# Splitting the first expert's weights: fewer pieces in the attention loop and all of them on GpSimd, the last three in the transition, and key tiles of half the size

## The chip, the cores and the metric

The kernel runs on one core of a Trainium2 chip. The metric is the device time of one execution in microseconds (us): median, lowest and highest of several runs. The profile is of one execution of its own. The core has a matrix engine (TensorE; PE in the profile, its weight loads PEld), a vector engine (VectorE, DVE), a scalar engine (ScalarE, ACT), GpSimd (POOL) and a queue engine (SyncE, SP) that mostly starts DMA transfers. Each engine runs its own instructions in the order in which they were written and waits on semaphores for the others. The matrix engine writes its results into PSUM, from which ScalarE and VectorE read; GpSimd works on SBUF alone.

## The reference

Attention with pooled keys and values, and then a mixture of eight experts of which each row takes one:

```
k_p = k.reshape(B, H, S // 8, 8, 64).mean(axis=3)       # v_p likewise; B = H = 8, S = 576
scores = q @ k_p.T / 8;  attn = softmax(scores)          # 72 pooled keys
x = (attn @ v_p) as (4608 rows, 512)
e = argmax(x @ w_gate)                                   # one of 8 experts for each row
out[row] = gate[row] * (relu(x[row] @ w1[e]) @ w2[e])    # w1[e] 512 x 1024, w2[e] 1024 x 512
```

## The kernel before

**Attention.** `attention` (L79 to L649) works on 36 tiles of 128 query rows, in four groups of nine (`NT` = 9; the number within the group is `KIND(t)`, L55). Two of the 8 sequences of `B` form one group. The program is written out by hand in the order in which each engine shall run it; the loop over `t` (L543) is a software pipeline. In one step, called tile t here, it does in this order:

- loads of later keys, values and queries by SP (L546 to L555), and the load of a raw weight piece (L565);
- `p_transpose(t)` (L278): TensorE transposes tile t's attention weights in six pieces (L283), ScalarE copies them out in two copies (`pt`, L284);
- `scores(t + 2)` (L257): 32 small matmuls into `pS` (L263), then on VectorE the maximum (`mx`, L267) and the subtraction (`sd`, L270), both read from PSUM;
- `q_transpose(t + 3)` (L250): four transposes and a copy by ScalarE;
- in some steps the transposes of the next group's pooled keys and values (`kv_transpose`, L176, with four copies by ScalarE) or the expansion of the values with the gate's columns (`v_expand`, L202, with one copy);
- `weights(t + 2)` (L274): the exponentials on ScalarE;
- `weigh(t)` (L291): TensorE multiplies the weights by the values into `pU` (L299), and `scale(t)` (L302) on VectorE divides by the sums (`r`, `lh`, `xe`, L311 to L315).

**Routing.** Tiles are routed in batches of three (`SIZES`, L38), the last of them at tiles 2, 5, ..., 20, 23, 26, 29, 32. `route` (L329) appends to VectorE's order: the logits' sum `rg` (L374), its maximum `rm` (L375), the difference `rd` (L376) and the key `rk` (L378) directly, and after the next tile's `mx` the maximum `rn` (L379) and the choice `ro` (L346). `rd`, `rk` and `ro` have two operands in SBUF. In the next tile, after `weigh`, TensorE counts the rows of each expert from `ro` (L356, L359), VectorE adds the carry (L361, L362), and GpSimd multiplies (`rp`, L388). One tile later VectorE reduces to the row numbers (`rf`, L389), and GpSimd scatters the batch to DRAM, for each tile one cast (`ix`, L368) and one indirect DMA (L407).

**The first expert's weights.** The experts' products are made in split form: a high part (`fp32r`, a cast by ScalarE) and a low part (raw minus high). The first expert's w1 and w2 are eight pieces of 128 x 1024 (512 KB each): pieces 0 to 3 are w1, 4 to 7 are w2. With `W0T` = 21, piece i is loaded by SP in tile 18 + i into one of four buffers that the raw keys and values use as well (`w_load`, L415). It is split at the end of tile 21 + i (`w_split`, L421): the cast on ScalarE (L424), the subtraction on GpSimd where the tile's number divides by 3 (pieces 0, 3, 6), else on VectorE (L425).

**The transition.** From tile 29 on, the first unit's rows are loaded back (`x_load`, L433, eight transfers by SP) and split (`x_split`, L450). `x_open` (L444), at tile 31, gives the memory of the buffers for raw data to the tiles `X` and `H`. After the loop TensorE runs six of eight hidden pieces of the first unit (`multiply`, L461, L463; each piece is 12 matmuls into one of three banks), and ScalarE and VectorE take out the first four (`hidden`, L467: L468, L469). In between VectorE computes the experts' tables (`plan`, L652), which calls `more_hidden` (L640) in the middle and `last_hidden` (L644) at its end. Then all engines meet at L728, where SP waits for each in turn, and `experts` (L712) begins: up to 16 units of at most 512 rows, with their own splits of later experts' weights (L1061 on ScalarE, L1069 on VectorE and GpSimd). At its start GpSimd clears `Y` (L1338).

**The keys.** `kTs` (L91) holds the pooled keys transposed, with the even heads in partitions 0 to 63 and the odd ones in 64 to 127. Each has its own 72 of 144 columns; the other 72 stay zero and are read by no matmul. VectorE clears the first of the two tiles at the start (L101), GpSimd the second (L493).

Of the kernel before, what the change touches and what calls it, by code (L numbers as in the profile page):

```python
# [10 lines left out]
F32 = mybir.dt.float32  # L11
# [4 lines left out]
ALU = mybir.AluOpType  # L16
AX = mybir.AxisListType

P = 128
# [3 lines left out]
SK = S // POOL  # L23
# [10 lines left out]
NB = 3  # L34
# [6 lines left out]
W0T = 21  # L41
# [9 lines left out]
def f32(a):  # L51
    return a.bitcast(F32)
# [26 lines left out]
def attention(ctx, outer, tc, q, k, v, wg, w1v, w2v, xs, W, cst, carry, tab, banks):  # L79
    nc = tc.nc  # L80
# [7 lines left out]
    e2 = early.enter_context(tc.tile_pool(name="e2", bufs=2, side="right", reuse_waits="tile"))  # L88
    kraw = early.enter_context(tc.tile_pool(name="akv", bufs=4, side="right", reuse_waits="tile"))

    kTs = [one.tile([P, 2, 4, 2 * SK], F32, name=f"kT{i}") for i in range(2)]  # L91
    kvp = e1.tile([P, NT, P], F32, name="kvp")
    vT = e1.tile([P, H * KP + KW], F32, name="vT")
    Vs = [one.tile([P, 2, 2, 5, D + NE + 1], F32, name=f"V{i}") for i in range(2)]
# [3 lines left out]
    colv = e1.tile([P, 5], F32, name="colv")  # L98
    exs = [one.tile([P, NB, NE + 1], F32, name=f"ex{i}") for i in range(2)]
    nc.vector.memset(kvp, 0.0)  # L100
    nc.vector.memset(kTs[0], 0.0)  # L101
    nc.vector.memset(vT, 0.0)

    for t in Ps:
# [71 lines left out]
    def kv_transpose(g, i, bank, what="kv", take=nc.scalar.copy):  # L176


        for c in range(3):
            nc.tensor.transpose(bank[:, c * P : (c + 1) * P], kvp[:, 3 * i + c, :], ident)  # L180
        m = bank[:, 0 : 3 * P].rearrange("p (c bj hp k) -> p hp bj k c", c=3, hp=2, k=8)
        for hp in range(2):
            rk, rv = slice(64 * hp, 64 * hp + 64), slice(64 - 64 * hp, 128 - 64 * hp)
            ko = kTs[g % 2].rearrange("p b j (hp k c) -> p hp (b j) k c", hp=2, c=9)
            vo = vT[:, 0 : 2 * H * KP].rearrange("p (bj hp x) -> p hp bj x", hp=2, x=KP)[:, :, :, 0:SK].rearrange("p hp b (k c) -> p hp b k c", c=9)
            if "k" in what:
                take(out=ko[rk, hp, :, :, 3 * i : 3 * i + 3], in_=m[0:64, hp])
            if "v" in what:
                take(out=vo[rv, hp, :, :, 3 * i : 3 * i + 3], in_=m[64:128, hp])

# [66 lines left out]
    def scores(t):  # L257
        g = t // NT
        for j in range(4):
            for p0, b in [(0, 0), (64, 1)] if KIND(t) == 4 else [(0, parts(t)[0][2]), (64, parts(t)[0][2])]:  # L260
                for hp in range(2):
                    r = slice(64 * hp, 64 * hp + 64)
                    nc.tensor.matmul(pS[p0 : p0 + 64, hp, j * SK : (j + 1) * SK], lhsT=qT[t][r, j * P + p0 : j * P + p0 + 64],  # L263
                                     rhs=kTs[g % 2][r, b, j, hp * SK : (hp + 1) * SK], start=True, stop=True, skip_group_check=True)
        s4 = pS[:, :, 0:288].rearrange("p a (h x) -> p a h x", h=4)
        mx = p2.tile([P, 2, 4], F32, tag="mx", name=f"mx{t}")
        nc.vector.tensor_reduce(out=mx, in_=s4, axis=AX.X, op=ALU.max)  # L267
        weave()
        sd = p2.tile([P, 2, 4, SK], F32, tag="sd", name=f"sd{t}")
        nc.vector.tensor_tensor(out=sd, in0=s4, in1=mx.unsqueeze(3).to_broadcast([P, 2, 4, SK]), op=ALU.subtract)  # L270
        weave(1, True)
        sds[t] = sd
# [140 lines left out]
    w0 = {}  # L413

    def w_load(i):  # L415

        raw = kraw.tile([P, 1024], F32, tag="raw", name=f"w0_{i}")
        nc.sync.dma_start(out=raw.rearrange("p (c f) -> p c f", c=4 if i < 4 else 2), in_=load_piece(w1v, w2v, 0, i))
        w0[i] = raw

    def w_split(i):  # L421
        raw = w0.pop(i)
        c, a = slice((i % 4) * 1024, (i % 4 + 1) * 1024), 0 if i < 4 else 2
        nc.scalar.copy(out=W[:, a, c], in_=raw)  # L424
        (nc.gpsimd if (W0T + i) % NB == 0 else nc.vector).tensor_tensor(out=W[:, a + 1, c], in0=raw, in1=f32(W[:, a, c]), op=ALU.subtract)  # L425

    def clear_rows():
        for s in range(4):  # L430
# [13 lines left out]
    def x_open():  # L444
        early.close()
        m1 = outer.enter_context(tc.tile_pool(name="m1", bufs=1, side="right", reuse_waits="tile"))
        u0["H"] = m1.tile([P, 2, 8, 512], F32R, name="H")
        u0["X"] = m1.tile([P, 2, 4, 512], F32R, name="X")

    def x_split(s):  # L450
        bank, o = (pm, pq)[s % 2], slice(s * P, (s + 1) * P)
# [9 lines left out]
    def multiply(n):  # L461
        for f, k, i in products[:n]:
            nc.tensor.matmul(pH[f % 3], lhsT=w1s(W[:, int(i == 2)], f, k), rhs=u0["X"][:, int(i == 1), k, :],  # L463
                             start=k + i == 0, stop=k == 3 and i == 2, skip_group_check=True)
        del products[:n]

    def hidden(f):  # L467
        nc.scalar.activation(out=u0["H"][:, 0, f, :], in_=pH[f % 3], func=AF.Relu)  # L468
        nc.vector.scalar_tensor_tensor(out=u0["H"][:, 1, f, :], in0=pH[f % 3], scalar=0.0, in1=f32(u0["H"][:, 0, f, :]), op0=ALU.max, op1=ALU.subtract)  # L469
# [20 lines left out]
    clear_rows()  # L490
    gate_rhs()
    sums()
    nc.gpsimd.memset(kTs[1], 0.0)  # L493

    def warm(n):
        for _ in range(n):
# [46 lines left out]
    for t in range(total):  # L543
# [14 lines left out]
        for at, n, *gj in adds:  # L558
            if at == t:
# [2 lines left out]
                    pieces[third] = kv_pool(*gj, vec)  # L562
                halves.extend(pieces[third][:n])
                del pieces[third][:n]
        if 0 <= t - W0T + 3 < 8:  # L565
            w_load(t - W0T + 3)
        if 0 < t < total - 2:
            p_transpose(t)
        if 2 < t + 2 < total:
# [41 lines left out]
        for bt, (t0, nb) in enumerate(batches):  # L611
            if t == t0 + nb - 1:
                route(bt)
        if 0 <= t - W0T < 8:
            w_split(t - W0T)
        if t == total - 7:
            x_load()
        if t == total - 5:
# [20 lines left out]

    def more_hidden():  # L640
        hidden(1)
        multiply(12)

    def last_hidden():  # L644
        for f in range(2, AF_EV):
            hidden(f)
            multiply(12)

    return u0, more_hidden, last_hidden  # L649
# [876 lines left out]
```

## Time and profile before

| | us |
|---|---|
| median of 3 runs | 627.91 |
| lowest, highest | 627.83, 630.01 |
| profiled execution, its own time | 627.27 |
| its span, first to last instruction | 625.7 |
| attention to the last step's x split and the transition, up to L860 | 0 to 188.76 |
| experts | 188.76 to 625.70 |

| engine | busy us | share of the span |
|---|---|---|
| PE | 599.4 | 96% |
| PEld | 511.0 | 82% |
| DVE | 347.9 | 56% |
| ACT | 241.4 | 39% |
| POOL | 241.7 | 39% |

A row of a timeline gives the start and the length in us from the span's start, the engine, the line, the operation, the tile that is written and those that are read with their shapes, how many instructions were merged, and in brackets how long the engine stood idle before and what ended that. A row of a source line's view gives the minimum, median and maximum length in ns, and the first and last start. A row by windows gives the busy time (and count) of each engine in a stretch.

### The profile page before, as it was taken

The numbers are of one execution on the slowest core, as the hardware profiler recorded it, in microseconds if no ns is written. First come the engines' busy times: TensorE is split into PE (matmuls) and PEld (weight loads), VectorE is DVE, ScalarE is ACT, GpSimd is POOL, SyncE is SP. The second block draws the span as 40 slices with busy tenths as digits, with TensorE's granted clock in tenths as the row PEclk, the third lists the DMA queues.
The fourth block names the chain that finished last, engine by engine and source line by source line (L and its number), as shares of the span: only waits on it lengthen the run. The fifth ranks groups of instructions, "written<-read, shape, count | busy, mean of one in ns | idle before, by whom it ended". The sixth has DMA issues, their size and how long they took to land.

```text
span 625.7 us, 13480 instructions
## 1 busy us (share of the span) xinstructions
PE 599.4 (96%) x4412; PEld 511.0 (82%) x4412; DVE 347.9 (56%) x731; ACT 241.4 (39%) x453; POOL 241.7 (39%) x288
## 2 busy tenths in 40 slices
PE   6989999999999999999999999999999999999995
PEld 5778989888877878789897888888898888888994
DVE  6699898888751324368475532755137764133220
ACT  2567776877411114065363411523024641021110
POOL 7447657644321122367444411152116861101101
PEclk9999999999999999999999999999999999999999
DMA  9999998982334931506967853064304353100001
GB/s 321 367 279 267 306 262 263 252 253 70 126 111 145 288 112 54 186 25 179 289 185 230 273 115 87 2 211 136 105 35 143 89 146 71 56 0 37 36 4 53
DMA packets 93938, 96.48 MB, mean 154 GB/s; under 512 B 43102, under 2 KB 74846, under 8 KB 93792
## 3 DMA queue, kind: packets, MB, share of 16 engines
q1 hardware_dynamic: 85808, 74.27, 42.3%
q0 software_dynamic: 7440, 20.50, 9.2%
q8 instruction: 61, 1.00, 0.7%
q14 instruction: 85, 0.70, 0.4%
q10 hardware_dynamic: 544, 0.02, 0.0%
HBM read 72.68 MB, written 26.00 MB: 158 GB/s over the span
## 4 chain that ended last, share of the span: by engine, by line
PE 76%; DVE 9%; issue 5%; POOL 4%; ACT 2%; DMA 2%; DVEq 0%; SPq 0%; ACTq 0%; POOLq 0%
PE pU L882 32%; PE pP L860 20%; PE pq L860 10%; PE pU L299 4%; DMA XE<-in_v_dram 2%; PE pP L283 2%; PE pP L463 2%; POOL dispatched L407 2%; PE pS L263 1%; PE pq L253 1%; DVE raw L172 1%; DVE mx L267 1%; POOL raw L172 1%; PE pm L207 1%; DVE xe L315 1%
## 5 line engine op out<-in xcount | busy, mean ns | idle before, releaser
L882 PE MATMUL pU<-W,H 128*128 128x512 f32 x912 | 216.3, 397 | 0.0
L882 PEld LDWEIGHTS pU<-W,H 128*128 128x128 f32 x912 | 171.3, 188 | 41.0
L860 PE MATMUL pP<-X,W 128*128 128x512 f32 (+3 forms) x748 | 143.2, 345 | 4.2 <-DVE W L1069 1.5
L860 PEld LDWEIGHTS pP<-X,W 128*128 128x128 f32 x748 | 122.7, 188 | 21.4 <-issue 3.0
L1351 POOL DMA_INDIRECT out_dram<-Y,GT x51 | 52.8, 1036 | 192.5 <-DVE Y L1174 179.3
L1069 POOL TENSOR_TENSOR W<-ST,W 128x1024 fp32r<-128x1024 f32 x30 | 77.8, 2607 | 88.1 <-ACT W L1061 88.1
L971 ACT ACTIVATE H<-pP 128x512 fp32r<-128x512 f32 (+1 forms) x67 | 36.0, 538 | 191.0 <-PE pP L860 154.7
L1174 DVE TENSOR_SCALAR Y<-pU,GT 128x512 f32<-128x512 f32 x36 | 27.0, 749 | 107.6 <-PE pU L882 106.2
L992 DVE SCALAR_TENSOR_TENSOR H<-pP,H 128x512 fp32r<-128x512 f32 (+2 forms) x73 | 42.2, 580 | 72.0 <-ACT H L971 70.3
L860 PE MATMUL pq<-X,W 128*128 128x512 f32 (+3 forms) x364 | 73.0, 348 | 2.4 <-issue 1.7
L860 PEld LDWEIGHTS pq<-X,W 128*128 128x128 f32 x364 | 60.0, 188 | 11.7 <-issue 2.5
L1061 ACT CAST W<-ST 128x1024 fp32r<-128x1024 f32 x56 | 57.3, 1054 | 6.7 <-DMA ST<-in_moe_w_dram 6.7
L299 PE MATMUL pU<-V,pt 110*128 110x146 f32 (+3 forms) x468 | 56.7, 283 | 1.4 <-ACT pt L284 0.8
L299 PEld LDWEIGHTS pU<-V,pt 110*128 110x128 f32 (+3 forms) x468 | 51.4, 179 | 3.1 <-ACT pt L284 1.8
L407 POOL DMA_INDIRECT dispatched<-xe,ix x36 | 39.8, 1107 | 18.2 <-POOL ix L368 9.8
L971 ACT ACTIVATE H<-pq 128x512 fp32r<-128x512 f32 (+1 forms) x33 | 17.9, 542 | 70.0 <-PE pq L860 68.5
L1069 DVE TENSOR_TENSOR W<-ST,W 128x1024 fp32r<-128x1024 f32 x26 | 40.5, 1560 | 4.6 <-ACT W L1061 4.1
L992 DVE SCALAR_TENSOR_TENSOR H<-pq,H 128x512 fp32r<-128x512 f32 (+2 forms) x35 | 20.8, 595 | 30.6 <-ACT H L971 29.8
L284 ACT COPY pt<-pP 110x384 f32<-110x384 f32 x72 | 30.9, 481 | 6.5 <-PE pP L283 5.8
L1049 DVE TENSOR_TENSOR X<-pS,X 128x512 fp32r<-128x512 f32 x34 | 21.9, 685 | 19.0 <-ACT X L1034 11.3
L276 ACT ACTIVATE P<-sd 128x576 f32<-128x576 f32 x36 | 24.8, 689 | 19.9 <-DVE sd L270 18.0
L172 POOL TENSOR_TENSOR raw<-raw 128x768 f32<-128x768 f32 (+1 forms) x18 | 26.3, 1460 | 13.5 <-DMA raw<-in_v_dram 12.8
(185 smaller groups left out, 625.4 us busy)
## 6 DMA issues: line engine op xcount, KB each, us to landing
ST<-in_moe_w_dram SPq DMA_DIRECT2D x56, 512.0 KB, 6.3
raw<-in_k_dram SPq DMA_DIRECT2D x12, 768.0 KB, 7.3
raw<-in_v_dram SPq DMA_DIRECT2D x11, 768.0 KB, 10.1
XE<-dispatched SPq DMA_DIRECT2D x104, 64.0 KB, 2.5
qa<-in_q_dram SPq DMA_DIRECT2D x24, 256.0 KB, 7.5
w<-in_moe_w_dram SPq DMA_DIRECT2D x8, 512.0 KB, 5.3
XE<-dispatched SPq DMA_DIRECT2D x15, 256.0 KB, 4.3
qa<-in_q_dram SPq DMA_DIRECT2D x2, 1024.0 KB
```

The lines of the kernel that those rows point to most:

```text
L172: return lambda: eng.tensor_tensor(out=out, in0=raw[:, :, 0:n], in1=raw[:, :, n : 2 * n], op=ALU.add)
L284: take(out=pt[t][a][0:R], in_=pPs[a][0:R, 0 : 3 * P])
L299: nc.tensor.matmul(pu[p0 : p0 + n, a, h * VW : (h + m) * VW], lhsT=pt[t][a][0:r, c % 3 * P + p0 : c % 3 * P + p0 + n], rhs=Vs[g % 2][0:r, ...
L407: apart(nc.gpsimd.indirect_dma_start(out=xs, out_offset=bass.IndirectOffsetOnAxis(ap=at, axis=0), in_=rows, in_offset=None))
L860: r = pe.matmul(out=pH[g % 3][:, :m], lhsT=w1s(w, f, k), rhs=x, start=i == 0, stop=i == len(passes) - 1)
L882: r = pe.matmul(out=pY[:, s % 2, :], lhsT=h, rhs=w[:, k * 512 : (k + 1) * 512], start=start and i == 0, stop=stop and i == len(ps) - 1, sk ...
L971: act.activation(out=HH[:, f, o], in_=src[:, o], func=AF.Relu).then_inc(Q["A_h"], 1)
L992: return dve.scalar_tensor_tensor(out=dst[:, f, to], in0=src[:, at], scalar=0.0, in1=f32(HH[:, f, at]), op0=ALU.max, op1=ALU.subtract)
L1061: act.copy(out=(W1H if i < 4 else W2H)[:, o], in_=ST[:, i, :]).then_inc(Q["A_s1" if i < 4 else "A_s2"], 1)
L1069: eng.tensor_tensor(out=(W1L if i < 4 else W2L)[:, o], in0=ST[:, i, :], in1=f32((W1H if i < 4 else W2H)[:, o]), op=ALU.subtract).then_inc( ...
L1174: r = dve.tensor_scalar(out=Y[:, s, :], in0=a, scalar1=gate, scalar2=None, op0=ALU.mult)
L1351: pool.indirect_dma_start(out=out, out_offset=bass.IndirectOffsetOnAxis(ap=GT[:, u, s, 1:2].bitcast(I32), axis=0), in_=Y[:, s, :], in_offs ...
```

## The change

1. Only pieces 0 to 4 are split in the loop, one every second tile: at the ends of tiles 21, 23, 25, 27 and 29, loaded three tiles ahead (18, 20, ..., 26). All five subtractions are on GpSimd.
2. Pieces 5, 6 and 7 are loaded by SP at tiles 32, 33 and 34 into a new tile `late`, which lies behind `H` and `X`. In the transition ScalarE casts piece 5 after the second hidden piece and pieces 6 and 7 after the third; VectorE subtracts 5 and 6 after the third hidden piece and 7 after the fourth.
3. Each key tile has 72 columns instead of 144: the even and the odd heads use the same columns in their own partitions. The two clears go.

```
-    kTs = [one.tile([P, 2, 4, 2 * SK], F32, name=f"kT{i}") for i in range(2)]
+    kTs = [one.tile([P, 2, 4, SK], F32, name=f"kT{i}") for i in range(2)]
-    nc.vector.memset(kTs[0], 0.0)
...
-            ko = kTs[g % 2].rearrange("p b j (hp k c) -> p hp (b j) k c", hp=2, c=9)
+            ko = kTs[g % 2].rearrange("p b j (k c) -> p (b j) k c", c=9)
-                take(out=ko[rk, hp, :, :, 3 * i : 3 * i + 3], in_=m[0:64, hp])
+                take(out=ko[rk, :, :, 3 * i : 3 * i + 3], in_=m[0:64, hp])
...
-                                     rhs=kTs[g % 2][r, b, j, hp * SK : (hp + 1) * SK], ...
+                                     rhs=kTs[g % 2][r, b, j, :], ...
...
-        raw = kraw.tile([P, 1024], F32, tag="raw", name=f"w0_{i}")
+        raw = kraw.tile([P, 1024], F32, tag="raw", name=f"w0_{i}") if i < 5 else u0["late"][:, i - 5]
...
-    def w_split(i):
-        raw = w0.pop(i)
-        c, a = slice((i % 4) * 1024, (i % 4 + 1) * 1024), 0 if i < 4 else 2
-        nc.scalar.copy(out=W[:, a, c], in_=raw)
-        (nc.gpsimd if (W0T + i) % NB == 0 else nc.vector).tensor_tensor(out=W[:, a + 1, c], in0=raw, in1=f32(W[:, a, c]), op=ALU.subtract)
+    def w_high(i):
+        nc.scalar.copy(out=W[:, 0 if i < 4 else 2, (i % 4) * 1024 : (i % 4 + 1) * 1024], in_=w0[i])
+
+    def w_low(i, eng):
+        c, a = slice((i % 4) * 1024, (i % 4 + 1) * 1024), 0 if i < 4 else 2
+        eng.tensor_tensor(out=W[:, a + 1, c], in0=w0.pop(i), in1=f32(W[:, a, c]), op=ALU.subtract)
...
+        u0["late"] = m1.tile([P, 3, 1024], F32, name="late")
...
-    nc.gpsimd.memset(kTs[1], 0.0)
...
-        if 0 <= t - W0T + 3 < 8:
-            w_load(t - W0T + 3)
+        if 0 <= t - W0T + 3 < 10 and (t - W0T + 3) % 2 == 0:
+            w_load((t - W0T + 3) // 2)
+        if 32 <= t < 35:
+            w_load(t - 27)
...
-        if 0 <= t - W0T < 8:
-            w_split(t - W0T)
+        if 0 <= t - W0T < 10 and (t - W0T) % 2 == 0:
+            w_high((t - W0T) // 2)
+            w_low((t - W0T) // 2, nc.gpsimd)
...
     def more_hidden():
         hidden(1)
+        w_high(5)
         multiply(12)
 
     def last_hidden():
         for f in range(2, AF_EV):
             hidden(f)
+            if f == 2:
+                w_high(6)
+                w_high(7)
+            for i in ((5, 6), (7,))[f - 2]:
+                w_low(i, vec)
             multiply(12)
```

More of the change, by code (lines that the diff above doesn't have):

```diff
@@ L263, in scores @@
                     nc.tensor.matmul(pS[p0 : p0 + 64, hp, j * SK : (j + 1) * SK], lhsT=qT[t][r, j * P + p0 : j * P + p0 + 64],
-                                     rhs=kTs[g % 2][r, b, j, hp * SK : (hp + 1) * SK], start=True, stop=True, skip_group_check=True)
+                                     rhs=kTs[g % 2][r, b, j, :], start=True, stop=True, skip_group_check=True)
         s4 = pS[:, :, 0:288].rearrange("p a (h x) -> p a h x", h=4)
```

## The prediction

> **What bounds the kernel now.** I read the page first, then busy time by stage, then by tile, then the chain of waits of the stretch in which the first expert's weights are split. In the table below the first eleven rows are attention tiles, cut where TensorE begins one tile's six transposes (L283); the row that starts at 115.24 is tile 22, the one at 148.74 tile 30, and the first row, for comparison, is tile 17. The last two are the transition and the experts. Columns: from:to, length, busy time and count on PE, PEld, DVE, ACT, POOL, then clock and DMA.
>
> ```profile
> 96.02:100.05 4.03, 4.03 (x62) 3.77 (x61) 3.45 (x7) 2.54 (x5) 3.39 (x6) 1.00 1.02 291
> 115.24:119.59 4.35, 3.95 (x75) 3.13 (x72) 3.82 (x12) 3.93 (x10) 2.12 (x3) 1.00 0.73 219
> 119.59:123.54 3.95, 3.95 (x60) 3.50 (x58) 3.10 (x7) 3.90 (x9) 3.22 (x5) 1.00 1.09 246
> 123.54:128.28 4.74, 3.89 (x60) 3.20 (x59) 4.57 (x13) 3.55 (x7) 1.60 (x3) 1.00 1.06 339
> 128.28:132.60 4.32, 4.29 (x64) 3.89 (x63) 3.25 (x10) 3.71 (x8) 2.26 (x3) 1.00 0.96 246
> 132.60:136.64 4.04, 4.04 (x62) 3.79 (x61) 3.62 (x7) 3.04 (x7) 3.12 (x5) 1.00 0.89 279
> 136.64:141.09 4.45, 4.33 (x67) 3.86 (x65) 4.08 (x12) 3.21 (x6) 1.89 (x3) 1.00 0.46 169
> 141.09:145.39 4.30, 4.30 (x64) 3.84 (x63) 3.38 (x11) 3.71 (x8) 2.26 (x3) 1.00 0.00 2
> 145.39:148.74 3.35, 3.35 (x56) 3.10 (x55) 3.11 (x7) 2.49 (x5) 2.70 (x4) 1.00 0.02 5
> 148.74:152.26 3.52, 3.52 (x61) 3.18 (x59) 3.35 (x12) 2.02 (x4) 2.30 (x4) 1.00 0.42 161
> 159.56:188.76 29.20, 26.82 (x181) 21.99 (x179) 19.20 (x90) 8.09 (x19) 10.43 (x17) 1.00 0.28 102
> 188.76:625.70 436.94, 425.35 (x2068) 357.69 (x2068) 193.37 (x301) 127.47 (x210) 137.44 (x98) 1.00 0.40 118
> ```
>
> TensorE is the bound nearly everywhere: 425 of 437 us in the experts, which the change does not touch. A plain tile takes 3.35 us (tile 29), one that also expands V takes 4.03 (tile 17). Tiles 22, 24, 25, 27 and 28 take more than their kind; in tile 24 ScalarE and VectorE are the long ones. The chain of waits (start, us, engine, instruction) names the splits there:
>
> ```profile
> 120.40 1.04 ACT W L424
> 121.46 1.23 DVE W L425
> ```
>
> **The change part by part.** The splits' price, from the rows of the raw pieces (instructions, then minimum, median and maximum in ns, first and last start):
>
> ```profile
> L418 SPq DMA_DIRECT2D w<-in_moe_w_dram x8: 368/554/1027, 97.4 to 133.1; - x8
> L424 ACT CAST W<-w x8: 1023/1030/1059, 116.3 to 145.5; 128x1024 fp32r<-128x1024 f32 x8
> L425 DVE TENSOR_TENSOR W<-w,W x5: 1216/1220/1226, 121.5 to 146.6; 128x1024 fp32r<-128x1024 f32 x5
> L425 POOL TENSOR_TENSOR W<-w,W x3: 2357/2361/2363, 117.8 to 143.5; 128x1024 fp32r<-128x1024 f32 x3
> ...
> DMA to landing us min/median/max: 3.8/5.3/8.1
> ```
>
> Removed from tiles 22 to 30: five VectorE splits (5 x 1.22 = 6.1 us of busy time) and three ScalarE casts. Tile 21's split stays, so tiles 22 and 23 keep their lengths: tile 22 still has its cast, and in tile 23 PE was busy throughout. If every stretched tile fell to its kind, the gain would end at 0.4 (22, PE's idle time) + 1.22 (24, against tile 30, which also counts a batch) + 0.29 + 0.42 + 0.27 = 2.6 us; I take less. Tile 24: ScalarE's key and value copies of tile 23 remain ahead of the cast. The cast that leaves tile 22's end frees 1.03 us there, of which waiting for the transposed queries takes back some 0.6, an estimate, so the cast in tile 24 ends about 0.45 earlier and TensorE's wait behind it shrinks by as much: 0.46. Tile 25: 4.32 to 4.05. Tile 27: its 4.45 holds a wait for the count's input behind a VectorE split, 0.3 goes. Tile 28: 4.30 to 4.07. Tiles 26 and 29 were at their kind; tile 30 gets a new cast that VectorE's earlier finish covers to 0.03. Without anything new that is -0.46 - 0.27 - 0.30 - 0.23 + 0.03 = -1.23 us.
>
> Something is new: GpSimd's 2.36 us splits now also stand at tiles 23, 25 and 29. Tiles 23 and 29 close a routing batch. VectorE then computes rd, rk and, after the next maximum, ro (L376, L378, L346), each from two operands in SBUF, and TensorE's count (L356) waits for ro with the next tile's transposes behind it. Before, GpSimd's splits stood at tiles 21, 24 and 27, away from these. What a GpSimd elementwise instruction does to such a VectorE instruction the trace shows:
>
> ```profile
> 38.61 3.09 POOL L172 TENSOR_TENSOR raw<-raw 128x768 f32<-128x768 f32 x2 [4.25 <-DMA raw<-in_v_dram]
> ```
> ```profile
> 41.35 0.39 DVE L376 TENSOR_TENSOR rd<-rg,rm 128x24 f32<-128x24 f32 x1
> ```
> ```profile
> L376 DVE TENSOR_TENSOR rd<-rg,rm x13: 166/182/386, 41.4 to 172.9; 128x24 f32<-128x24 f32 x11, 128x16 f32<-128x16 f32 x1, 128x8 f32<-128x8 f32 x1
> ```
> ```profile
> L1069 DVE TENSOR_TENSOR W<-ST,W x26: 1206/1226/3130, 249.5 to 505.7; 128x1024 fp32r<-128x1024 f32 x26
> ```
> ```profile
> L315 DVE TENSOR_TENSOR xe<-pU,r x35: 678/681/692, 30.1 to 171.9; 128x512 f32<-128x512 f32 x35
> ```
>
> GpSimd's pair of adds ended at 41.70; the rd that began under it ended at 41.74 and took 0.39 instead of 0.18. The experts' split took up to 3.13 instead of 1.23, so 1.9 us can be lost at once. Instructions that read PSUM (L315) never vary, so mx, sd and xe pass. I therefore let rd, rk or ro wait until GpSimd's split ends. The Trainium skill says so outright (SBUF — State Buffer, section "SBUF: two separate sides": VectorE and GpSimd share a port pair that one of them holds for a whole instruction, and a VectorE instruction with two SBUF inputs needs it against a GpSimd one that reads SBUF). For an instruction as short as rd this trace shows only 0.21 us lost; with that much per catch the sum would stay a gain of 0.8, while with the page's rule it becomes the loss below.
>
> Where the splits fall. Tile 24, VectorE's, TensorE's and ScalarE's own order of time:
>
> ```profile
> 125.63 0.18 DVE L376 TENSOR_TENSOR rd<-rg,rm 128x24 f32<-128x24 f32 x1
> 125.84 0.18 DVE L378 SCALAR_TENSOR_TENSOR rk<-rd,order 128x24 f32<-128x24 f32 x1
> ...
> 127.95 0.18 DVE L346 TENSOR_TENSOR ro<-rk,rn 128x24 bf16<-128x24 f32 x1
> ```
> ```profile
> 128.18 0.17 PE L356 MATMUL pm<-ro,lstrict 128*128 128x24 bf16 x1
> ```
> ```profile
> 124.84 1.02 ACT L424 CAST W<-w 128x1024 fp32r<-128x1024 f32 x1
> ```
>
> With the cast 0.45 earlier it ends at 125.4 and GpSimd's split runs from 125.5 to 127.85. VectorE, without its split at 121.46, is 0.3 earlier: rd 125.3, rk 125.5, then mx, then ro near 126.5. So either rk waits (ro starts 0.9 after it, which is 127.95 - 125.84 less the 1.22 of the split between them, so at 128.75, and the next transposes start 0.33 after ro: 129.1) or rk slips through and ro waits (127.95, transposes at 128.28). Against 128.28 before, that is +0.85 or 0.0 instead of -0.46; I take +0.4. Tile 30:
>
> ```profile
> 150.62 0.98 POOL L407 DMA_INDIRECT dispatched<-xe,ix  x1 [0.28 <-POOL ix L368]
> ```
>
> The batch's last scatter ends at 151.60, 2.86 after the tile's start at 148.74. It had been held by a VectorE split at tile 28 that goes, so I put the new split's start 1.5 to 2.8 us into the tile. By tile 24's spacing rd comes at 1.8, rk at 2.0, ro at 2.9: one is caught in that whole range. Caught at rk from 1.6, the next transposes start at 1.6 + 2.36 + 0.9 + 0.33 = 5.2; caught at ro from 2.2, at 2.2 + 2.36 + 0.43 = 5.0 (0.1 for ro to start). Against 3.52 that is +1.5 to +1.7; I take +1.6. Tile 23's split ends before the next batch's product on GpSimd (rp, L388), and tile 25's before the pick of tile 26 or a few tenths into it, so 0.1 at most reaches TensorE there. Sum: +0.4 - 0.27 - 0.30 - 0.23 + 1.6 = +1.2 us.
>
> The transition adds three VectorE splits (3.66 us) and three casts (3.09). All engines meet before the experts, and SP's wait there shows who is last:
>
> ```profile
> SPq L728 <- PE pq L463: 4.2, 1, 4.2
> ```
> ```profile
> 182.33 0.69 DVE L469 SCALAR_TENSOR_TENSOR H<-pP,H 128x512 fp32r<-128x512 f32 x1 [1.51 <-ACT H L468]
> ```
> ```profile
> POOL Y L1338 <- issue: 10.8, 1, 10.8
> ```
> ```profile
> 178.86 5.60 PE pP L463 x24
> ```
>
> VectorE's last piece ends at 183.02; TensorE's last product is awaited 4.2 us longer, to 187.2. VectorE was idle for 1.51 us before 182.33, so it now ends at 183.02 + 3.66 - 1.51 = 185.17: 2.1 us of cover remain. GpSimd is idle for the 10.8 us before L1338, so nothing holds these splits. Hidden pieces come 2.8 us apart (5.60 for two); a hidden piece and two casts take 0.6 + 2.06 on ScalarE, so the casts fit. The tables of the plan come ahead of the splits. Cost 0; without the cover, up to 3.66. Their loads go onto SP behind the row loads:
>
> ```profile
> 157.28 1.12 SPq L437 DMA_DIRECT2D GT<-dispatched  x1
> ```
>
> From 158.4, three issues of at most 1.03 and 8.1 to landing end at 169.6; the first late cast follows the second hidden piece, two pieces before the 182.3 above, so 176.7. SP's next issue behind them, the clearing of rows, waits for the last batch's carry anyway. Fewer weight buffers in use at once can only shorten SP's waits.
>
> The keys: same number of columns per matmul and elements per copy, so 0. The two clears (about 1 us each) end ahead of waits for data:
>
> ```profile
> 5.74 0.96 DVE L172 TENSOR_TENSOR raw<-raw 128x768 f32<-128x768 f32 x1 [0.31 <-DMA raw<-in_k_dram]
> ```
> ```profile
> 23.39 1.82 POOL L172 TENSOR_TENSOR raw<-raw 128x768 f32<-128x768 f32 x1 [5.32 <-DMA raw<-in_v_dram]
> ```
>
> VectorE and GpSimd wait for DMA right after them, so 0; without that cover 1 us would be gained.
>
> The profiled execution took 627.27 us, 0.64 below the median of the runs (627.91). It should become 628.5, and the median 629.1.
>
> **The rivals.** First, the short VectorE instructions lose next to nothing (0.21 in one row is all the trace has of them), or GpSimd's splits fall beside them: then the -1.23 stands and the median is 626.7, at best 625.3 with all 2.6. For it: windows of a few tenths at tile 24. Against: at tile 30 the target is 1.3 us wide. Second, slower: the transition's cover fails. It decides once three splits take over 3.66 + 2.1 = 5.8 us, 1.9 each; at the experts' worst, 3.13 each, they take 9.4, and the meeting comes 3.6 later, median 632.7. Against it: those long ones ran under GpSimd, which is idle here.
>
> **How the numbers follow.** Forecast 0.55; first rival 0.30, of which 0.04 for a gain past 0.5% by a cover or clear that I priced at nothing; second rival 0.08; small shifts without a name, within 0.5%, 0.07. A measurement can tell about 0.5% of this kernel, 3.1 us, from no change. So faster 0.04, same 0.55 + 0.26 + 0.07 = 0.88, slower 0.08. The range goes from 626.0, near the first rival's gain, to 631.2: both catches at rk with longer splits (+2.2) and a run spread like before's, whose highest is 630.01.
>
> **What would show it.** Right: under GpSimd's splits of tiles 23 and 29 one of rd, rk, ro lasts 1 to 2.4 us; tile 30 lasts about 5 us and waits for ro; tiles 25, 27 and 28 last 4.05 to 4.15; the stretch to SP's meeting shifts as a whole; VectorE's late splits take 1.22 and end before TensorE. Wrong: no such long instruction and tile 31 beginning by 151.2; or TensorE idle at the meeting with VectorE last; or a change inside the experts.

## The result, and the profile after

The changed kernel is slower. Its median is 632.87 us (629.1 to 635.0, 14 runs), against 628.0 (625.23 to 633.01, 14 runs) for the kernel before, run in turn with it. The ratio is 1.0076 [1.0057, 1.0096], 4.9 us on the medians. The forecast was 629.1, at most 631.2. The profiled execution took 634.09 us (span 632.5). In the changed kernel the lines of the attention are one lower (L283 is L282, L346 is L345) and those of the experts seven higher (L860 is L867); the cast is L421, the subtraction L425.

The stretches as in the prediction's table (tiles 23, 24, 25, 27, 28, 30 and 31, then transition and experts), in the kernel after:

```profile
119.76:123.49 3.73, 3.73 (x60) 3.48 (x58) 2.58 (x6) 3.29 (x9) 2.98 (x6) 1.00 0.30 72
123.49:128.91 5.42, 3.88 (x61) 3.20 (x59) 5.05 (x11) 3.17 (x6) 3.43 (x3) 1.00 1.02 264
128.91:132.98 4.07, 4.07 (x64) 3.82 (x63) 3.25 (x10) 3.33 (x8) 0.55 (x3) 1.00 0.99 294
...
137.02:141.95 4.93, 4.33 (x66) 3.86 (x65) 4.56 (x11) 1.90 (x4) 3.35 (x2) 1.00 0.30 110
141.95:146.19 4.24, 4.24 (x64) 3.84 (x63) 3.38 (x11) 3.71 (x8) 2.26 (x3) 1.00 0.01 2
...
149.55:155.15 5.60, 3.72 (x61) 3.20 (x59) 5.23 (x11) 2.71 (x5) 3.89 (x4) 0.98 0.28 105
155.15:159.99 4.84, 4.84 (x71) 3.99 (x69) 3.33 (x10) 2.58 (x6) 0.55 (x3) 0.68 0.88 224
...
163.86:193.11 29.25, 26.83 (x181) 21.99 (x179) 22.51 (x93) 10.93 (x22) 8.13 (x14) 1.00 0.32 112
193.11:632.50 439.39, 425.36 (x2068) 357.70 (x2068) 198.54 (x301) 127.44 (x210) 139.39 (x98) 1.00 0.39 117
```

Tiles 24, 27 and 30 are stretched (by 0.68, 0.48 and 2.08 us against before), tiles 23 and 25 shortened (0.22 and 0.25), and tile 31 takes 4.84 instead of 3.43. In the three stretched tiles PE is busy 3.88, 4.33 and 3.72 us of the length: it waits. In tile 31 it is busy throughout, but the clock column says 0.68: it works slowly. By the start of the experts 4.35 us have gathered (193.11 against 188.76). Inside the experts it is 2.45 more in these two executions, of which more below.

The waits have one cause. Call the routing's operations for one batch, `rg` to `ro`, its pick. The picks of the batches that end with tiles 23, 26 and 29 lie in the stretches of tiles 24, 27 and 30. GpSimd's subtraction at each of the three (before the second, the first of the scatters behind which it waits its turn), and the VectorE instruction that stands under it, for the last one with what follows:

```profile
125.40 2.35 POOL L425 TENSOR_TENSOR W<-w,W 128x1024 fp32r<-128x1024 f32 x1 [0.55 <-ACT W L421]
...
134.22 1.02 POOL L406 DMA_INDIRECT dispatched<-xe,ix  x1 [1.75 <-DVE xe L386]
...
138.18 2.37 POOL L425 TENSOR_TENSOR W<-w,W 128x1024 fp32r<-128x1024 f32 x1
...
151.39 2.36 POOL L425 TENSOR_TENSOR W<-w,W 128x1024 fp32r<-128x1024 f32 x1
```
```profile
125.48 2.31 DVE L377 SCALAR_TENSOR_TENSOR rk<-rd,order 128x24 f32<-128x24 f32 x1
...
138.79 1.80 DVE L375 TENSOR_TENSOR rd<-rg,rm 128x24 f32<-128x24 f32 x1
...
151.32 2.48 DVE L375 TENSOR_TENSOR rd<-rg,rm 128x24 f32<-128x24 f32 x1
153.83 0.18 DVE L377 SCALAR_TENSOR_TENSOR rk<-rd,order 128x24 f32<-128x24 f32 x1
153.94 0.75 DVE L266 TENSOR_REDUCE mx<-pS 128x8 f32<-128x576 f32 x1
154.60 0.17 DVE L378 TENSOR_REDUCE rn<-rk 128x3 f32<-128x24 f32 x1
154.81 0.18 DVE L345 TENSOR_TENSOR ro<-rk,rn 128x24 bf16<-128x24 f32 x1
```

In tile 30 `rd`, 0.18 us of work, takes 2.48 and ends 0.05 after GpSimd's subtraction. In tile 24 it is `rk` (2.31), in tile 27 `rd` (1.80); each ends 0.04 after its subtraction. TensorE's timeline shows who waits:

```profile
128.81 0.17 PE L355 MATMUL pm<-ro,lstrict 128*128 128x24 bf16 x1 [1.23 <-DVE ro L345]
...
141.84 0.19 PE L355 MATMUL pm<-ro,lstrict 128*128 128x24 bf16 x1 [0.60 <-DVE ro L345]
...
155.04 0.18 PE L355 MATMUL pm<-ro,lstrict 128*128 128x24 bf16 x1 [1.88 <-DVE ro L345]
```

At the longest wait the granted clock falls. The first row is the first 1 us of tile 31:

```profile
155.15:156.15 1.00, 1.00 (x9) 1.00 (x8) 0.96 (x4) 0.46 (x1) 0.00 (x0) 0.50 0.86 246
...
158.15:159.15 1.00, 1.00 (x14) 0.83 (x14) 1.00 (x3) 0.46 (x1) 0.00 (x0) 0.93 0.99 255
```

In finer windows the clock is at 0.50 from 154.88, just before the wait ends, to 158.29: 3.4 us.

The transition kept its length (29.20 and 29.25). SP's wait at the meeting, and VectorE's late splits:

```profile
SPq L735 <- PE pq L462: 2.4, 1, 2.4
SPq L735 <- DVE W L425: 2.2, 1, 2.2
```
```profile
L425 DVE TENSOR_TENSOR W<-late,W x3: 1220/1220/1224, 185.0 to 187.9; 128x1024 fp32r<-128x1024 f32 x3
```

SP waits first for VectorE's last piece and then another 2.4 us for TensorE's product: TensorE is still last, and the late splits cost nothing.

### The profile page after: what moved, and what is told of

Same layout as the page of the kernel before. It is cut to its first block, busy times and chain, and to the rows that moved or that the text cites. A ratio compares the mean times of both kernels' runs of the same rounds, so it can differ in the third digit from the quotient of the medians.

```text
span 632.5 us, 13470 instructions
## 1 busy us (share of the span) xinstructions
PE 601.3 (95%) x4412; PEld 512.8 (81%) x4412; DVE 355.1 (56%) x728; ACT 242.0 (38%) x453; POOL 245.5 (39%) x289
## 4 chain that ended last, share of the span: by engine, by line
PE 69%; issue 8%; DVE 8%; POOL 7%; DMA 4%; SPq 2%; ACT 1%; DVEq 0%; ACTq 0%; POOLq 0%
PE pU L889 31%; PE pP L867 19%; PE pq L867 9%; POOL dispatched L406 3%; PE pU L298 2%; DMA XE<-in_v_dram 2%; POOL raw L171 2%; PE pP L462 2%; DMA ST<-in_moe_w_dram 1%; SPq L227 1%; PE pP L282 1%; PE pS L262 1%; DMA raw<-in_k_dram 1%; DVE xe L314 1%; POOL ix L367 1%
## 5 line engine op out<-in xcount | busy, mean ns | idle before, releaser
L867 PE MATMUL pP<-X,W 128*128 128x512 f32 (+3 forms) x748 | 143.2, 345 | 4.9 <-DVE W L1076 2.3
L867 PEld LDWEIGHTS pP<-X,W 128*128 128x128 f32 x748 | 122.8, 188 | 21.7 <-issue 3.0
L867 PE MATMUL pq<-X,W 128*128 128x512 f32 (+3 forms) x364 | 73.1, 348 | 3.0 <-DVE H L999 1.6
L867 PEld LDWEIGHTS pq<-X,W 128*128 128x128 f32 x364 | 59.9, 188 | 12.7 <-DVE H L999 2.5
L1076 DVE TENSOR_TENSOR W<-ST,W 128x1024 fp32r<-128x1024 f32 x26 | 46.3, 1781 | 4.8 <-ACT W L1068 4.8
L406 POOL DMA_INDIRECT dispatched<-xe,ix x36 | 37.8, 1049 | 14.6 <-POOL ix L367 9.2
L283 ACT COPY pt<-pP 110x384 f32<-110x384 f32 x72 | 30.9, 478 | 7.7 <-PE pP L282 7.0
L266 DVE TENSOR_REDUCE mx<-pS 128x8 f32<-128x576 f32 x36 | 27.1, 752 | 7.8 <-PE pS L262 7.8
```

Source lines behind the costliest of these rows:

```text
L283: take(out=pt[t][a][0:R], in_=pPs[a][0:R, 0 : 3 * P])
L406: apart(nc.gpsimd.indirect_dma_start(out=xs, out_offset=bass.IndirectOffsetOnAxis(ap=at, axis=0), in_=rows, in_offset=None))
L867: r = pe.matmul(out=pH[g % 3][:, :m], lhsT=w1s(w, f, k), rhs=x, start=i == 0, stop=i == len(passes) - 1)
L1076: eng.tensor_tensor(out=(W1L if i < 4 else W2L)[:, o], in0=ST[:, i, :], in1=f32((W1H if i < 4 else W2H)[:, o]), op=ALU.subtract).then_inc( ...
```

## The experiments

My theory after the result: a GpSimd subtraction that reads SBUF holds every VectorE instruction with two SBUF operands that comes up under it; that is the whole loss up to tile 30; and the long wait lowers TensorE's clock. The rivals: the late pieces or the keys cost the time; GpSimd's mere activity does it; the clock falls for another reason.

There were four comparisons, each on one chip with its own runs of the kernel before (medians 626.66, 632.46, 632.97 and 626.24). In the second and third the kernel before was some 6 us longer, and in the third the changed kernel 8 to 10, because VectorE and ScalarE began late in some tiles (below); so only ratios within a comparison are compared. A ratio stands with its 95% interval in brackets and is not exactly the quotient of the two medians.

### First comparison: which part of the change

**e1_low_on_vector.** Three subtractions go to VectorE, where GpSimd would work under a pick.

```
-            w_low((t - W0T) // 2, nc.gpsimd)
+            w_low((t - W0T) // 2, nc.gpsimd if t in (21, 27) else vec)
```

> The changed kernel, with the subtractions of tiles 23, 25 and 29 on VectorE instead of GpSimd; the casts stay where the change puts them, and the transition and the keys are those of the change. Theory 1 (GpSimd's subtraction holds the routing's rd or rk, which have two operands in SBUF): the holds at tiles 24 (2.31 us), 27 (1.81) and 30 (2.48) are gone, every rd and rk is 0.18, tiles 24, 27 and 30 fall from 5.42, 4.93 and 5.60 to under 4.8, 4.3 and 3.9, tile 31 from 4.84 to 3.45, and the median is within 1.5 us of before (628). Rival (the casts at the ends of tiles 23, 25 and 29 come between the exponentials and the copies of the transposed weights and make those tiles long): tiles 24 and 30 stay over 5 us and the median near 632.9.

626.06 us, ratio 0.9998 [0.9975, 1.0022]. Tiles 24, 27, 30 and 31 take 4.43, 4.16, 4.43 and 3.43. VectorE at the pick that lasted longest above:

```profile
148.77 0.18 DVE L375 TENSOR_TENSOR rd<-rg,rm 128x24 f32<-128x24 f32 x1
148.99 0.18 DVE L377 SCALAR_TENSOR_TENSOR rk<-rd,order 128x24 f32<-128x24 f32 x1
149.09 1.22 DVE L425 TENSOR_TENSOR W<-w,W 128x1024 fp32r<-128x1024 f32 x1
```

The split still stands ahead of `ro`, but as 1.22 us of VectorE's own work and not as 2.36 of GpSimd's. For that tile 30 stays above the 3.9 us expected; the other tiles and the median came as expected. The whole loss goes with the three instructions; everything else of the change, the casts at the same places too, is still in this kernel.

**e2_keys_alone.** The kernel before with the small key tiles and without the two clears, and nothing else.

```
-    kTs = [one.tile([P, 2, 4, 2 * SK], F32, name=f"kT{i}") for i in range(2)]
+    kTs = [one.tile([P, 2, 4, SK], F32, name=f"kT{i}") for i in range(2)]
-    nc.vector.memset(kTs[0], 0.0)
...
-    nc.gpsimd.memset(kTs[1], 0.0)
```

> The kernel before with the key tiles of half the size and without their two clears, nothing else. Theory 1: nothing on the path changes, within 0.5 us of before. Rival (another placement of the copies' output or of everything behind it in SBUF slows the small matmuls or the copies): L262's matmuls or the key copies are longer than 223 ns and 0.35 us, and the median is 1 to 4 us above before.

627.49 us, ratio 0.9996 [0.9973, 1.0019]; the tiles are those of before to 0.01 us. The keys and the clears do nothing that can be measured.

**e3_late_pieces.** The changed kernel, with pieces 0 to 4 split as before at tiles 21 to 25.

```
-        if 0 <= t - W0T < 10 and (t - W0T) % 2 == 0:
-            w_high((t - W0T) // 2)
-            w_low((t - W0T) // 2, nc.gpsimd)
+        if 0 <= t - W0T < 5:
+            w_high(t - W0T)
+            w_low(t - W0T, nc.gpsimd if t % NB == 0 else vec)
```

> The changed kernel with pieces 0 to 4 split where the kernel before splits them (tiles 21 to 25, GpSimd at 21 and 24, VectorE at 22, 23 and 25); pieces 5 to 7 stay in the transition. Theory 1: tile 24 as before (4.7), tiles 27 and 28 without a split, 0.4 us shorter together; VectorE's late splits 1.22 each and TensorE last at the meeting; median 0.3 to 1.0 us below before, 627.0 to 627.7. Rival (the transition's splits or the late loads cost what the change lost): SP's meeting is later after the last tile than before, and the median is 2 to 4 us above before.

626.01 us, ratio 0.999 [0.9972, 1.0008]. SP waits for TensorE 2.4 us after VectorE at the meeting here too. The late pieces cost nothing; they take the splits out of tiles 27 and 28 (4.16 and 4.06 us instead of 4.45 and 4.30), which is too little to be measured.

**e4_free_tiles.** The five pieces are split at the ends of tiles 21, 24 and 27 (GpSimd) and 25 and 28 (VectorE), none behind a tile that closes a batch.

```
+        if t in (21, 24, 25, 27, 28):
+            i = (21, 24, 25, 27, 28).index(t)
+            w_high(i)
+            w_low(i, nc.gpsimd if t % NB == 0 else vec)
```

> The changed kernel with its five pieces at the ends of tiles 21, 24 and 27 on GpSimd (just after the product rp, where no rd, rk or ro follows within 2.4 us) and of tiles 25 and 28 on VectorE (in tiles without routing); three pieces in the transition. Theory 1: no rd, rk or ro over 0.2 us, tile 24 near 3.6, 25 near 4.2, 27 near 4.15, 30 near 3.5; the stretch to the experts is 1.5 to 2.2 us shorter than before, median 625.8 to 626.5. Rival (what costs is the number of pieces in the loop, or the transition): like the changed kernel or before, 628 to 633.

624.45 us, ratio 0.9964 [0.994, 0.9988]: the lowest ratio of all, and a gain on the kernel before. Tiles 24, 27 and 30 take 3.46, 4.15 and 3.50, and the experts begin at 186.31. GpSimd's splits are as long as ever:

```profile
L425 POOL TENSOR_TENSOR W<-w,W x3: 2353/2353/2360, 117.6 to 140.8; 128x1024 fp32r<-128x1024 f32 x3
```

So it matters where they fall and not how long they are.

### Second comparison: what of GpSimd's instruction holds VectorE

**e5_clears** and **e8_copies** put another GpSimd instruction in the place of the subtraction for pieces 1, 2 and 4: one that only writes SBUF, and one that reads and writes it. Both leave out the low parts of these pieces, e5 the high parts too; e8 puts copies of the high parts there.

```
+        if i in (1, 2, 4):
+            w0.pop(i)
+            nc.gpsimd.memset(f32(W[:, a : a + 2, c]), 0.0)                     # e5
+            nc.gpsimd.tensor_copy(out=W[:, a + 1, c], in_=f32(W[:, a, c]))     # e8
+            return
```

> The changed kernel, but at the ends of tiles 23, 25 and 29 GpSimd clears both parts of the piece (128 x 2048, a write that reads nothing, about 1.8 us) after the cast instead of subtracting; the first expert's pieces 1, 2 and 4 are thus left out of the products. Theory 1 in the form of a held read port: rd and rk stay at 0.18 although GpSimd is busy over them, tiles 24, 27 and 30 have no hold. Rival (any GpSimd work on SBUF holds them): one of rd, rk or ro lasts 1 to 1.8 us at tiles 24 and 30.

> The changed kernel, but at the ends of tiles 23, 25 and 29 GpSimd copies the high part into the low part (one operand read, about 1 us) instead of subtracting; the low parts of pieces 1, 2 and 4 of the first expert are thus wrong copies. If one operand that GpSimd reads is enough for the hold, rd or rk under it lasts until the copy ends, up to 1 us; if it takes GpSimd's two operands, all are 0.18.

One execution each: 636.73 and 633.63 us. GpSimd and VectorE at tile 24 in e5:

```profile
131.24 1.80 POOL L427 MEMSET W<- 128x2048 f32 x1 [2.39 <-ACT W L421]
```
```profile
131.17 0.18 DVE L377 SCALAR_TENSOR_TENSOR rk<-rd,order 128x24 f32<-128x24 f32 x1
...
132.14 0.18 DVE L345 TENSOR_TENSOR ro<-rk,rn 128x24 bf16<-128x24 f32 x1
```

and in e8:

```profile
131.18 1.04 POOL L427 CAST W<-W 128x1024 fp32r<-128x1024 f32 x1 [1.98 <-ACT W L421]
```
```profile
131.33 0.93 DVE L375 TENSOR_TENSOR rd<-rg,rm 128x24 f32<-128x24 f32 x1
```

Under the clear, `ro` takes its 0.18 us; under the copy, `rd` takes 0.93 and ends 0.04 after it. In tile 30 of e5 even all three, `rd`, `rk` and `ro`, lie under the clear (160.19 to 161.99) and take 0.18. GpSimd's activity alone does not hold VectorE; its reading of SBUF does. The length of tile 30 shows it too: 5.42 us in e5, against 7.09 in e6 of the same comparison, where a subtraction stands there. Tile 24's lengths (7.36 in e5, 5.76 in e8) do not, because a late start in tile 23 and, in e5, a slow clock lie in them (below).

**e6_filled_wait** puts 14 transposes of TensorE ahead of the count at tile 30, **e7_last_piece_at_30** splits the last loop piece behind tile 30 instead of 29.

```
+        if t == 30:                                                            # e6
+            for _ in range(14):
+                nc.tensor.transpose(pPs[0][:, 0:P], ident, ident)
...
-        if 0 <= t - W0T < 10 and (t - W0T) % 2 == 0:                           # e7
+        if t in (21, 23, 25, 27, 30):
```

> The changed kernel with 14 transposes of the identity on TensorE (into a bank whose content is not read again before it is written anew) between tile 30's product and its count, so that TensorE is busy for about 1.8 us of its wait for ro. Theory of the clock (the granted clock fell to 0.50 after TensorE stood idle for 1.9 us): tile 30 stays at about 5.6, tile 31 falls from 4.84 to 3.45 at a clock of 1.00, and the median is 1.4 us below the changed kernel's, near 4 us above before. Rival (tile 31 is long by its own work or by the routing behind it): tile 31 stays near 4.8.

> The changed kernel with piece 4 split at the end of tile 30 instead of 29, its load as before at tile 26; nothing else. Theory 1: tile 30 falls from 5.60 to 3.5 and tile 31 from 4.84 to 3.45, the holds of tiles 24 and 27 stay; median 3.5 us below the changed kernel's, 1.0 to 1.5 us above before. Rival (the number of GpSimd splits counts, not the place): no change against the changed kernel.

e6: 645.72 us, ratio 1.0188 [1.0143, 1.0233]. e7: 640.95, ratio 1.0115 [1.0077, 1.0153]. Both missed. In e6 the transposes did fill the wait for `ro` in tile 30 (they end at 162.80, the count starts at 162.85), and the clock was 1.00 in tile 31. But in e9 below, the same kernel without them, it is 1.00 there as well, behind a wait of 1.57 us: nothing was tested. In e7 tile 24 took 7.17 us and the gain at tile 30 (5.41, tile 31 4.12) could not be told from the rest. Part of e6's further loss lies past the tiles: a wait of 2.58 us at L892 that only e6 and e10 have in that size, put down to "issue".

### Third comparison: the same kernels once more

**e9_after_again** is the changed kernel, **e10_filled_again** is e6's, **e12_before_again** is the kernel before, and **e11_29_on_vector** moves one subtraction:

```
+            w_low((t - W0T) // 2, nc.vector if t == 29 else nc.gpsimd)
```

> The changed kernel once more, unaltered. Theory (GpSimd's subtraction holds the pick's small VectorE operations, and the longest of the waits also costs TensorE its clock): ratio to before 1.006 to 1.010; tiles 24, 27 and 30 at about 5.4, 4.9 and 5.2 to 5.7 us with one of rd, rk and ro stretched to 1.8 to 2.5 us in each; tile 31 at 4.8 us if the granted clock falls behind tile 30's wait, at 3.43 us if it stays at 1.00. Rival (the loss belonged to one chip or one execution): a ratio within 0.5% of 1, tile 31 at 3.43 us.

> The changed kernel with 14 filler transposes (about 1.7 us of TensorE work into a free PSUM bank) at tile 30 ahead of the count that waits for the pick. If the fall of the clock behind that wait is what lengthens tile 31: tile 31 at 3.43 us with a clock of 1.00, and 1.0 to 1.4 us less than the unaltered changed kernel beside it, if there the clock falls. Rival (the clock falls for another reason): tile 31 at 4.8 us here too. Third: the fillers only shift what follows and the kernel becomes longer than the changed one, as by 8 us against the kernel before in the first try of it.

> The changed kernel with one edit: the subtraction behind tile 29 runs on VectorE, the four others stay on GpSimd. Theory: nothing holds tile 30's pick, tile 30 at 4.4 us (as with three of them on VectorE) and tile 31 at 3.43 us with a clock of 1.00; that is 1.2 us less than the changed kernel, and 2.6 us less if the clock falls there; tiles 24 and 27 as in the changed kernel. Rival (it is not the overlap with the pick but GpSimd's load as a whole): tile 30 stays over 5 us.

> The kernel before, unaltered, with its trace taken on the same chip. If tiles have the lengths of the first trace on any chip: tiles 24, 27, 30 and 31 at 4.74, 4.45, 3.52 and 3.43 us. If some chips start VectorE's scores 1.4 to 2.1 us late at the tiles where a batch is picked: one or more of tiles 24, 27 and 30 at 5 us or more with no subtraction of GpSimd near.

e9: 640.74 us, ratio 1.01 [1.0067, 1.0132], as expected, but with tiles 24 and 30 longer than expected. e10: 645.84, 1.015 [1.0096, 1.0204]. e11: 638.88, 1.0075 [1.0045, 1.0105]. e12, in one execution: 631.92. The trace of e12 shows what is different here. VectorE and ScalarE in tile 30 of the kernel before:

```profile
155.99 0.76 DVE L267 TENSOR_REDUCE mx<-pS 128x8 f32<-128x576 f32 x1 [1.01 <-PE pq L253]
156.04 0.58 ACT L255 COPY qT<-pq 128x512 f32<-128x512 f32 x1 [1.42 <-PE pq L253]
```

TensorE's scores had ended at 154.07 in this trace, and yet neither engine began until 156. In the first trace `mx` began 0.83 us behind the scores, here 1.92, and tile 30 took 3.52 us and not 4.61. The same kernel has tiles 24 and 27 at 4.75 and 4.45, as ever. So neither of the two cases in its expectation came about as it stands.

The late starts need this setting: from tile 15 on, no trace of the first result and of the first and fourth comparisons has VectorE idle and over 0.3 us late on the scores. But the change has a part in them. The kernel before is late at tiles 15, 18 and 30. All seven traces of the changed kernel and its variants here (e5 to e11) are late at tiles 23, 26 and 29 too, by 1.1 to 1.9 us, where e12 starts as the first trace of before did. So a part of what the change costs more in this setting is not the hold.

Against e12, e9's tile 24 takes 7.67 (+2.92), tile 25 5.66 (+1.34), tile 27 4.94 (+0.49), tile 30 7.09 (+2.48). The hold is there in tiles 24 (`ro`, 1.78) and 30 (`rd`, 1.89), but almost gone in tile 27, where `rd` takes 0.34. VectorE and GpSimd at e9's tile 24:

```profile
130.67 0.75 DVE L266 TENSOR_REDUCE mx<-pS 128x8 f32<-128x576 f32 x1
131.34 0.17 DVE L378 TENSOR_REDUCE rn<-rk 128x3 f32<-128x24 f32 x1
131.54 1.78 DVE L345 TENSOR_TENSOR ro<-rk,rn 128x24 bf16<-128x24 f32 x1
```
```profile
130.94 2.34 POOL L425 TENSOR_TENSOR W<-w,W 128x1024 fp32r<-128x1024 f32 x1 [2.71 <-ACT W L421]
```

Three VectorE instructions run under one subtraction (130.94 to 133.28). `mx` reads PSUM, `rn` has one SBUF operand, and both keep their lengths; `ro`, with two, waits to the end. The Trainium skill has this rule (SBUF — State Buffer, section "SBUF: two separate sides": the port pair that both share is locked for a whole instruction, and a VectorE instruction needs it with two SBUF inputs, only against a GpSimd one that reads SBUF). e5, e8 and this row agree with each clause of it.

Yet in this tile 24 the hold costs nothing. TensorE waits for ScalarE's copy `pt`, which the late start in tile 23 has put off, and then works at half clock, so that the count comes with no wait, 1 us after `ro` is free:

```profile
131.41 3.17 PE L298 MATMUL pU<-V,pt 110*128 110x146 f32 x12 [1.62 <-ACT pt L283]
134.37 0.23 PE L355 MATMUL pm<-ro,lstrict 128*128 128x24 bf16 x1
```

The same product takes 1.71 us in the first trace. The +2.92 and tile 25's +1.34 are thus the late start and the clock. In tile 30 the hold does cost: the count waits 1.57 us for `ro`, while in e5, which starts as late there (1.89 us, 1.88 in e9), the count does not wait and the tile takes 5.42.

In e11 tile 30's `rd` and `rk` are back to 0.18 us and the count's wait falls from 1.57 to 1.00; the tile takes 6.50 instead of 7.09. By its number (over 5 us, not the 4.4 expected) the rival would be right, by its rows it is wrong: what is left is the late start and VectorE's own split. e10 is 5 us longer than e9, as its third case had it, and tile 31 takes 3.43 us in both: again no test of the clock.

### Fourth comparison: the clock, and the loss and the best version once more

**e13_filled_24** puts the filler where e9 had waited; **e14_low_on_vector_again** and **e15_free_tiles_again** are e1's and e4's kernels, **e16_after_third** is the changed kernel.

```
+        if t == 24:
+            for _ in range(10):
+                nc.tensor.transpose(pU[:, 1, 0:P], ident, ident)
         weigh(t)
```

> The changed kernel with 10 filler transposes (about 1.2 us of TensorE work into the bank of the next product) at tile 24 ahead of the product with V. On a chip like the last one TensorE waits about 1.6 us there and then runs at a clock of 0.50 to 0.70 through tile 25 (5.66 us instead of 4.07). If the wait is what lowers the clock: clock 1.00 in tiles 24 and 25, tile 25 at 4.07 us, 1.3 us or more less than the unaltered changed kernel beside it. Rival (the clock falls for another reason, power or the instructions' kind): tile 25 over 5 us as before. On a chip like the first one the wait lies behind the fillers and the kernel is up to 1.2 us longer.

> The changed kernel with the subtractions of tiles 23, 25 and 29 on VectorE, on another chip. If the loss there comes from GpSimd's subtractions under the pick too: a ratio to before of 0.997 to 1.003, no rd, rk or ro over 0.3 us at tiles 24, 27 and 30. Rival (on such a chip the late pieces or the other edits cost the time): a ratio of 1.005 or more.

> The version with the pieces split behind tiles 21, 24 and 27 on GpSimd and 25 and 28 on VectorE, three late. Theory: faster than before on this chip too, ratio 0.994 to 0.999, the start of the experts 1.5 to 2.5 us sooner than with e14. Rival: its gain belonged to the first chip, ratio 0.999 to 1.003.

> The changed kernel unaltered, the measure for the three others: ratio 1.006 to 1.013; a wait of TensorE of 1.3 us or more at tile 24 or 30 followed by a clock of 0.5 to 0.7 over 2.5 to 4 us, if the wait is the cause in at least one of them.

e16: 630.7 us, ratio 1.0067 [1.004, 1.0094]. e14: 625.54, 0.9997 [0.9977, 1.0018]. e15: 624.12, 0.9963 [0.9945, 0.9982]. So the first comparison is repeated in both: without the three holds no loss, with the splits in free tiles a gain (from tile 22 on e15 reaches the experts 1.84 us sooner than e14). e13: 631.89, 1.007 [1.0044, 1.0096]. There were no late starts here, so the wait that it was to fill was not there, and tile 25 took 4.07 in e13 and e16 alike. But e16 shows something else. Its count at tile 30, and its tile 31:

```profile
155.33 0.17 PE L355 MATMUL pm<-ro,lstrict 128*128 128x24 bf16 x1 [1.88 <-DVE ro L345]
```
```profile
155.46:158.89 3.43, 3.43 (x71) 2.81 (x68) 3.22 (x10) 2.27 (x6) 0.45 (x3) 1.00 0.81 216
```

The wait of the first trace to the hundredth, and no fall of the clock, against the expectation: tile 31 takes 3.43 us. In e13, behind 1.87 us, it takes 4.99. The same program with the same wait loses 1.4 us in one execution and nothing in the other.

## Why the prediction was wrong, point by point

The mechanism was right, and so was the sign, but the sum was a quarter of the loss. Two steps failed: where tile 25's split would fall, and the clock, which the sum has at nothing without a reason. Tile 30's term was too small. Times below are from tile 22 on, where the changed kernel was already 0.17 us later.

- **Tile 24, +0.4 taken.** The transposes of tile 25 start 0.63 later (128.91 against 128.28), 0.46 without the 0.17. Of the two branches the one with `rk` caught came about, but it had been priced at +0.85. That the middle of the branches, +0.4, was hit is luck.
- **Tile 25, -0.27.** Right: -0.25.
- **Tile 27, -0.30. This step failed.** It came to +0.48. The prediction had tile 25's split end "before the pick of tile 26 or a few tenths into it, so 0.1 at most reaches TensorE there". It began at 138.18, behind the batch's three scatters, which stand ahead of it on GpSimd and start only at 134.22, after 1.75 us of waiting for VectorE's `xe` (both rows stand above). So it lay 1.16 us into tile 27, over `rd`. For tile 30 the prediction had asked for the end of the last scatter; for tile 25 it had not. That is 0.8 us.
- **Tile 28, -0.23.** -0.06.
- **Tile 30, +1.6.** The mechanism was right, the size was not: +2.08. The split began 1.84 us into the tile, within the window given (1.5 to 2.8), but the price went by the earliest catch, 1.6. By the rows `rd`, not `rk`, was caught (it had begun 0.07 us before), and from its end to the next transposes the whole of `rk`, `mx`, `rn`, `ro` and the count follows, 1.35 us.
- **Tile 31, not in the sum. This step failed too.** The prediction followed TensorE's waits to the end of tile 30 and took the clock behind them as unchanged; it came to +1.41 in this execution. Together 0.46 - 0.25 + 0.48 - 0.06 + 0.01 + 2.08 + 1.41 = 4.13, against 1.2. Of the 2.9 us that the sum lacks the clock is half, tile 27 a quarter, tile 30 and tile 28 the rest.
- **The transition, the late loads, the keys: 0.** Right, by e2, e3 and SP's waits. The cover of 2.1 us that was worked out is 2.4 in the trace, so the second rival fell.
- **The experts, no change.** Not contradicted. The changed kernel's three profiles have 439.39, 440.69 and 437.4 us there, those of the kernel before 436.94 and 436.55, those of e1, e3, e4, e14 and e15 435.1 to 437.4. But e2, in which the experts and the splits are those of before, has 438.46, so single executions differ by as much. In the first pair the largest single difference is a wait of TensorE for VectorE's split (2.3 us against 1.5). The comparison below leaves some 0.5 us for this part, an estimate (3.3 less 2.78).

By e16's trace, which has the three holds and no fall of the clock, the experts begin 3.23 us later than in the first trace of before, 2.78 counted from tile 22. The medians of that comparison are 4.5 us apart. The mean granted clock, which is on record for each run, shows where the rest goes. At 0.996 and above the changed kernel has a median of 628.7 us (5 runs) and the kernel before 625.5 (19 runs); at 0.994 and 0.995 it is 631.1 (4) against 627.7 (11). So at an equal clock they are 3.2 to 3.4 us apart. The other 1.2 go with the clock: three of the twelve changed runs lie below 0.994, none of the thirty of before. One fall of 3.4 us to half clock takes 0.0027 off the mean of a run of 630 us.

It is not shown that the wait causes the fall: no filler stood where an unfilled kernel beside it had a fall. What speaks for it is only that in tiles 22 to 31, over all the traces, eight of the ten waits of 1.3 us and more had the clock at about 0.5 behind them, and that in the ten of these traces with no such wait, or with only e16's, the clock stayed at 1.00 throughout.

The first rival (no hold) is refuted by `rd` at 2.48 us. Its -1.23 was not a bad price for moving the splits away, though: e4 and e15, which place them otherwise and avoid the holds, gain 2.1 to 2.2 us on the medians of their comparisons.

## What to carry to other kernels

Before work is moved to GpSimd, lay its start, behind everything that stands ahead of it in GpSimd's own queue, over the short two-operand instructions of VectorE that TensorE waits for: a 0.18 us instruction there costs up to the whole length of GpSimd's (2.31 and 2.48 us under 2.35 and 2.36 here). Move such work in time rather than to another engine; the same 2.36 us subtraction was free where no pick followed. And where TensorE is the bound, give a wait of over 1.3 us a chance of a slower clock behind it; here a tile behind such a wait became 1.4 to 1.6 us longer where the clock fell.

## What the runs showed of the hardware that I had not expected

The granted clock fell to 0.50 at eight waits of 1.34 to 1.88 us, and did not at another of 1.88 (e16) nor at one of 1.57 (e9, tile 30). Six of the falls lasted 3.4 us, two (e5, e9) 6.8, twice that. They set in between 0.3 us before the wait's end (e5) and 1.3 us after it (e13). The Trainium skill (TensorE: Matmul & The Clock Gate, section "Part 1: The HAM clock gate (the "warmup" mystery)") has the clock set by windows of about 3.4 us that run freely, not in step with the program. The lengths of the falls, their loose distance to the wait, and that the same wait counts in one execution and not in another agree with that. That a wait of half a window is enough is not what its "idle window" says: no wait in these tiles was longer than 1.88 us, and here the measurement decides.

In two of four comparisons VectorE and ScalarE both began 1.1 to 2.1 us after TensorE's results were finished by the trace, at two early tiles in every kernel, at tile 30 in the kernel before and at tiles 23, 26 and 29 in the changed ones. The kernel before took 632 to 633 us there instead of 626 to 628. One chip showed it in one comparison and not in another. What it is was not tried; since the ends of matmuls in a trace are modelled, it is also open whether the engines began late or the results came late.
